# Scores of the first batch from undivided float32 over 64 rows, and one ring of seven staging buffers

## The chip, the cores and the metric

The kernel runs on one core of a Trainium2 chip. The metric is the device time of one execution in microseconds (us). Five engines work side by side, each through its own list of instructions in order: TensorE (PE, with its weight loads shown as PEld), VectorE (DVE), ScalarE (ACT), GpSimd (POOL) and SyncE (SP), which here issues nearly all DMAs.

## The reference, cut to what matters

Three stages follow each other: attention that keeps only the 32 largest scores of a row, a dense feed-forward layer, and a mixture of eight experts with two of them for each token.

```python
def _attn_ref(q, k, v):                        # (4 batches, 8 heads, 576, 64)
    scores = scale * np.matmul(q, k.transpose(0, 1, 3, 2))
    kth = np.partition(scores, -top_k, axis=-1)[..., -top_k:-top_k + 1]   # top_k = 32
    scores = np.where(scores >= kth, scores, -1000000000.0)
    ...
    return np.matmul(attn, v)

def reference(**kwargs):
    attn_out = _attn_ref(**attn_kwargs)
    x = attn_out.transpose(0, 2, 1, 3).reshape(B * S, H * D)    # 2304 x 512
    x = _moe_ref(x=x, **moe_kwargs)      # max(x @ w_in, 0)**2 @ w_out, inner width 2048
    return _moe2_ref(x=x, **moe2_kwargs)  # top 2 of 8 experts, inner width 1024
```

## The kernel before, in words

**Attention.** Work goes by units: one tile of 128 queries and one pair of heads; the 64 queries that are left of each batch's 576 make smaller "left" units. Batch 0 has units 0 to 19 of 80, the last four of them left units. For each head of a unit TensorE makes a score tile of 128 x 576 (line 439, in `scores`), ScalarE copies it out (442), VectorE searches it for its 32 largest values (453 to 494, some 28 instructions a head), ScalarE and GpSimd make the mask and the exponent (506 to 512), TensorE transposes (523) and multiplies by V (564).

**Divided operands.** TensorE's fp32r products take a reduced float32, so q and k are divided in a high part (ScalarE, line 400) and a low rest (line 401, VectorE or GpSimd, in `split`). The 64 rows of a head stand twice over the 128 partitions: `prep_k` puts the high part of k in rows 0 to 63 and its rest in rows 64 to 127, `prep_q` makes one tile of the high part of q and one of its rest, each over all 128 rows. A score tile is the sum of two fp32r products over 128 rows, each in two halves of 288 columns: four matmuls a head. The undivided k arrives in `kn` (two buffers, line 409), the undivided q in `qn` (two buffers, line 424). For batch 0 the first four heads of k and the first and third load of q are divided on VectorE, the rest on GpSimd.

**The feed-forward layer beside it.** Its weights arrive as 64-bit words and are turned to float32 by `convert`, 32 times: a load into `raw` (four buffers, line 147), two passes on ScalarE (153, 157), two on VectorE (155, 156), one on GpSimd (158), and a store to `whole` (159). The layer runs in chunks of token tiles. Chunk 0 (tiles 0 and 1) uses `whole` as plain float32 (loads at 333, products at 351 and 315). Chunk 1 loads `whole` again into `raw` (336), divides it (340, 341) and stores the parts in `wsc` (342), which the later chunks load.

**Order.** The program is written with priorities; a scheduler fixes each engine's list beforehand. Between the pieces of a unit the feed-forward matmuls of the chunk that is due are put in by a pace that counts them. SP issues DMAs in the order of its list, and an issue that has to wait for a buffer holds all behind it. The zero fills of `xs` and `out` (lines 136, 139) and the conversions stand on the same list as the loads of q, k and v. When attention is over, the rest of the feed-forward layer and then the experts run on TensorE.

Of the kernel before, what the change touches and what calls it, by code (L numbers as in the profile page):

```python
# [32 lines left out]
LAST_WAIT = 8  # L33
EXPERT_WAIT = 60
EARLY = 3
SOON = 300
# [18 lines left out]
def attention_ffn_moe(ctx: ExitStack, tc: tile.TileContext, q, k, v, w_ffn, w_route, noise, w_exp, out,  # L55
# [86 lines left out]


    def convert(vpool, f, which):
        n = DM
        raw = vpool.tile([P, 2 * n], U32, name="raw", bufs=4 if keep is not None else 2)
        nc.sync.dma_start(raw, w_ffn[f, which])
# [153 lines left out]
    def ffn(t0, nt, xT):  # L301
# [24 lines left out]
        for f in range(NF):  # L326
# [7 lines left out]
            elif divide:  # L334
                raw = vpools[0].tile([P, 2 * DM], U32, name="raw", bufs=4 if keep is not None else 2).bitcast(F32)
                nc.sync.dma_start(raw, whole[f].rearrange("p a d -> p (a d)"))
                for i, (w, eng) in enumerate(((wi, nc.gpsimd), (wo, nc.vector))):
                    part = raw[:, i * DM:(i + 1) * DM]
                    with prompt():
                        nc.scalar.activation(w[:, 0, :], part, AF.Copy)  # L340
                        eng.tensor_tensor(w[:, 1, :], part, w[:, 0, :].bitcast(F32), op=ALU.subtract)
                    nc.sync.dma_start(wsc[f][:, i], w.bitcast(F32))
            else:
                nc.sync.dma_start(wi.bitcast(F32), wsc[f][:, 0])
                nc.sync.dma_start(wo.bitcast(F32), wsc[f][:, 1])
# [57 lines left out]
    def prep_k(b, g, j):  # L403
# [3 lines left out]
        for h in ([2 * j], [2 * j + 1]) if (b, g) == (0, 0) else ([2 * j, 2 * j + 1],):  # L407
            kn = apool.tile([P, 2, S], F32, name="kn", bufs=2)[:, 0:len(h), :]
            nc.sync.dma_start(kn, k[b, 4 * g + h[0]:4 * g + h[-1] + 1].rearrange("h p s -> p h s"))
            dst = K4[b, g][:, h[0]:h[-1] + 1, :]  # L410
            for i in range(len(h)):
                split(nc.vector if (b, g) == (0, 0) else nc.gpsimd, dst[:, i], dst[:, i], kn[:, i], D)

# [7 lines left out]
    def prep_q(b, g, s0):  # L421

        qn = apool.tile([P, 4, P], F32, name="qn", bufs=2)
        nc.sync.dma_start(qn.rearrange("p h s -> p (h s)"), q[b, s0 // P, g])
        qt = apool.tile([P, 2, 4, P], F32R, name="qt", bufs=3)
        split(nc.vector if b == 0 and s0 == 0 else nc.gpsimd, qt[:, 0], qt[:, 1], qn, 0)
        return qt

    def scores(pairs, sb, whole, then):


        ps = ps_s.tile([P, 2, 512], F32, name="ps")
        for i, (st, kt, par) in enumerate(pairs):
            for n in range(2):
                if whole:
                    at, w = n * HS, HS
                else:
                    at, w = ((LEFT * par, NFULL * P), (0 if par else NFULL * P, LEFT))[n]
                nc.tensor.matmul(ps[:, n, 0:w], st, kt[:, at:at + w], start=(i == 0), stop=(i == len(pairs) - 1))  # L439
        with tc.high_priority(SOON):  # L440
# [127 lines left out]
    def pair_full(b, j, qt):  # L568

        hA = 2 * j  # L570
        q0 = 2 * (j % 2)
        sm = apool.tile([P, 2], F32, name="sm", bufs=6)
        e = apool.tile([P, 2 * S], F32, name="sb", bufs=4)
        for i in range(2):
            kt = K4[b, j // 2][:, (hA + i) % 4]
            sb = e[:, i * S:(i + 1) * S]
            scores([(qt[:, 0, q0 + i, :], kt, i), (qt[:, 1, q0 + i, :], kt, i)], sb, True,
                   lambda w, m, sb=sb, one=sm[:, i:i + 1]: softmax(sb, w, m, one))
            yield
# [9 lines left out]
    def pair_left(b, j, qt):  # L589
        hA = 2 * j  # L590
        q0 = 2 * (j % 2)
        st = []
        for i in range(2):
            kt = K4[b, j // 2][:, (hA + i) % 4]
            st += [(qt[:, 0, q0 + i, :], kt, i), (qt[:, 1, q0 + i, :], kt, i)]
        sm = apool.tile([P, 2], F32, name="sm", bufs=6)
# [7 lines left out]

        scores(st, e, False, then)
        yield
# [521 lines left out]
```

## Time and profile before

| | us |
|---|---|
| median of 3 runs | 1338.55 (1336.74 to 1340.67) |
| the profiled execution | 1336.86 |
| its span in the trace | 1335.1 |
| PE busy, share of the span | 1241.5 (93%) |
| DVE busy | 899.2 (67%) |
| ACT busy | 856.6 (64%) |
| POOL busy | 746.2 (56%) |

The busy time of a whole span says little here, since the stages have different limits: VectorE is the fullest engine in the first 200 us, TensorE from about 400 us on. The rest of the profile is read by stretch: the slices of the page, the busy time of each engine in stretches of 50 us, then the instructions around the places that the change touches, and what they waited for.

### The profile page before, as it was taken

How to read it: one execution, taken by the hardware profiler on the slowest of the kernel's cores; microseconds unless marked ns; L12 is line 12 of the kernel's file. 1: busy time of each engine (PE TensorE's matmuls, PEld its weight loads, DVE VectorE, ACT ScalarE, POOL GpSimd, SP SyncE). 2: the span in 40 equal slices, each digit the busy share in tenths (PEclk: the TensorE clock that was granted, in tenths of full speed). 3: DMA queues.
4: the chain of work that ended last, by engine and by line, in shares of the span. 5: the costliest groups of instructions: out<-in, count | busy, mean ns of one | idle time of the engine just before them, and what ended most of it. 6: DMA issues, size and time to landing. Idle time of an engine off the chain costs nothing.

```text
span 1335.1 us, 26136 instructions
## 1 busy us (share of the span) xinstructions
PE 1241.5 (93%) x8030; PEld 1071.8 (80%) x8030; DVE 899.2 (67%) x4557; ACT 856.6 (64%) x1886; POOL 746.2 (56%) x1243
## 2 busy tenths in 40 slices
PE   3769889989998999999999999999999999999997
PEld 2556667777887888888888888899899999988886
DVE  8999989998986899978677410255534343444554
ACT  6878879989897889987878653543433333332443
POOL 5857798887786676767655635333432241503221
PEclk9889999999999999999999999999999999999999
DMA  9998886875675554366534689366643443534464
GB/s 333 361 368 292 274 273 235 309 260 181 219 231 193 166 174 157 106 211 204 168 115 158 205 297 332 113 198 197 192 151 117 143 136 119 174 103 143 141 202 140
DMA packets 93302, 270.06 MB, mean 202 GB/s; under 512 B 11612, under 2 KB 11740, under 8 KB 93152
## 3 DMA queue, kind: packets, MB, share of 16 engines
q1 hardware_dynamic: 83872, 239.91, 54.3%
q0 software_dynamic: 9280, 28.40, 5.9%
q8 instruction: 65, 1.06, 0.3%
q14 instruction: 85, 0.70, 0.2%
HBM read 209.90 MB, written 60.45 MB: 202 GB/s over the span
## 4 chain that ended last, share of the span: by engine, by line
PE 61%; ACT 13%; DVE 11%; DMA 7%; issue 5%; POOL 3%; SPq 0%; POOLq 0%; DVEq 0%; ACTq 0%
PE pa L564 5%; PE ph L693 5%; PE ph L695 4%; PE ph L694 4%; PE acc L676 4%; PE acc L674 4%; PE acc L675 4%; PE ps L439 4%; PE pa L523 3%; PE acc L322 3%; PE acc L320 3%; PE acc L321 3%; DMA raww<-in_exp 3%; PE pf L357 2%; PE pf L358 2%
## 5 line engine op out<-in xcount | busy, mean ns | idle before, releaser
L511 POOL TENSOR_TENSOR sb<-sb,w 128x576 f32<-128x576 f32 x144 | 205.8, 1430 | 63.3 <-ACT w L510 59.3
L453 DVE MAX8 m<-sb 128x8 f32<-128x115 f32 (+1 forms) x720 | 190.3, 264 | 53.1 <-ACT sb L442 47.6
L457 DVE MATCH_REPLACE8 w<-m,sb 128x115 f32<-128x115 f32 (+1 forms) x720 | 187.1, 263 | 0.0
L699 ACT ACTIVATE ht<-ph 128x384 fp32r<-128x384 f32 (+1 forms) x128 | 55.8, 436 | 195.2 <-PE ph L695 177.0
L715 POOL DMA_INDIRECT out<-y,info x40 | 45.1, 1127 | 242.4 <-DVE y L714 224.7
L439 PE MATMUL ps<-K,qt 128*128 128x288 f32 (+2 forms) x640 | 131.4, 333 | 43.9 <-ACT sb L442 30.0
L700 DVE SCALAR_TENSOR_TENSOR ht<-ph,ht 128x384 fp32r<-128x384 f32 (+1 forms) x128 | 62.7, 490 | 161.7 <-ACT ht L699 148.5
L693 PE MATMUL ph<-xe,wi 128*128 128x256 f32 (+1 forms) x512 | 159.9, 312 | 1.9 <-ACT wi L686 1.0
L695 PE MATMUL ph<-xe,wi 128*128 128x256 f32 (+1 forms) x512 | 159.2, 311 | 0.2 <-DVE wi L687 0.2
L694 PE MATMUL ph<-xe,wi 128*128 128x256 f32 (+1 forms) x512 | 158.9, 310 | 0.0
L439 PEld LDWEIGHTS ps<-K,qt 128*128 128x128 f32 x640 | 103.7, 204 | 64.4 <-ACT sb L442 37.7
L512 ACT ACTIVATE sb<-sb,keep 128x576 f32<-128x576 f32 x144 | 112.5, 781 | 28.1 <-POOL sb L511 27.6
L674 PE MATMUL acc<-wo,ht 128*128 128x512 f32 x320 | 125.8, 397 | 0.4 <-DVE y L714 0.4
L675 PE MATMUL acc<-wo,ht 128*128 128x512 f32 x320 | 125.3, 395 | 0.0
L510 ACT ACTIVATE w<-sb,keep 128x576 f32<-128x576 f32 x144 | 111.3, 775 | 16.4 <-POOL keep L506 16.2
L371 POOL TENSOR_TENSOR gt<-r,gt 128x384 fp32r<-128x384 f32 (+1 forms) x96 | 90.7, 946 | 53.2 <-ACT gt L370 39.9
L481 DVE MAX8 m<-w 128x8 f32<-128x288 f32 x288 | 116.0, 443 | 0.1
L357 PE MATMUL pf<-xT,wi 128*128 128x384 f32 (+1 forms) x320 | 106.0, 331 | 5.4 <-ACT r L364 3.9
L523 PE MATMUL pa<-ident,sb 128*128 128x128 f32 x576 | 94.8, 289 | 16.5 <-ACT sb L512 7.1
L676 PE MATMUL acc<-wo,ht 128*128 128x512 f32 x320 | 108.9, 401 | 0.0
L525 ACT COPY pt<-pa 128x512 f32<-128x512 f32 x144 | 83.2, 578 | 32.1 <-PE pa L523 21.2
L693 PEld LDWEIGHTS ph<-xe,wi 128*128 128x128 f32 x512 | 96.4, 188 | 8.5 <-ACT wi L686 1.4
(211 smaller groups left out, 3511.9 us busy)
## 6 DMA issues: line engine op xcount, KB each, us to landing
raww<-in_exp SPq DMA_DIRECT2D x88, 512.0 KB
wi<-wsc SPq DMA_DIRECT2D x64, 512.0 KB
wo<-wsc SPq DMA_DIRECT2D x64, 512.0 KB
raw<-in_ffn SPq DMA_DIRECT2D x32, 512.0 KB
xs<-xr SPq DMA_DIRECT2D x40, 258.0 KB
mr<-xs SPq DMA_DIRECT2D x40, 258.0 KB
qn<-in_q SPq DMA_DIRECT2D x40, 256.0 KB
whole<-ca SPq DMA_DIRECT2D x32, 256.0 KB
```

What stands on the lines that cost most here:

```text
L357: nc.tensor.matmul(ph[:, 0:n], wi[:, 0, sl], xT[:, 0, c, 0:n], start=(c == 0), stop=False)
L439: nc.tensor.matmul(ps[:, n, 0:w], st, kt[:, at:at + w], start=(i == 0), stop=(i == len(pairs) - 1))
L453: in_turn(nc.vector.max(parts[i][1], sb[:, parts[i][0]]))
L457: in_turn(nc.vector.match_replace(out=w[:, sl], in_to_replace=top, in_values=sb[:, sl], imm_value=NEG))
L511: nc.gpsimd.tensor_tensor(sb, sb, w, op=ALU.subtract)
L523: nc.tensor.transpose(pt[:, c * P:(c + 1) * P], e[:, c * P:(c + 1) * P], ident)
L674: queued(nc.tensor.matmul(acc[t], hs[i][:, 0, sl], wo[:, 0, :], start=(f == 0), stop=False))
L675: queued(nc.tensor.matmul(acc[t], hs[i][:, 0, sl], wo[:, 1, :], start=False, stop=False))
L676: queued(nc.tensor.matmul(acc[t], hs[i][:, 1, sl], wo[:, 0, :], start=False, stop=(f == NFE - 1)))
L693: queued(nc.tensor.matmul(ph[:, 0:n], wi[:, 0, sl], xe[i][:, 0, c, :], start=(c == 0), stop=False))
L694: queued(nc.tensor.matmul(ph[:, 0:n], wi[:, 0, sl], xe[i][:, 1, c, :], start=False, stop=False))
L695: queued(nc.tensor.matmul(ph[:, 0:n], wi[:, 1, sl], xe[i][:, 0, c, :], start=False, stop=(c == NC - 1)))
```

## The change

For batch 0 (`WHOLE_BATCHES = 1`) q and k are loaded undivided straight into the tiles that TensorE reads, `qt` and `K4`, and nothing of them is divided. A head's score tile is one plain float32 product over 64 rows in place of two fp32r products over 128; its two halves of columns are taken from different rows, the first from rows 0 to 63 and the second from rows 64 to 127, where q and k stand twice. The later batches are computed as before. Their q and k, and the `raw` tiles of the conversions and of chunk 1, now take their staging buffers from one ring of seven tiles of 4 KB a partition (`staged`); before, `raw` had four of them, `kn` two of 4.5 KB and `qn` two of 2 KB. k of the later batches is loaded one head at a time instead of two.

```diff
+WHOLE_BATCHES = 1
+    def staged():
+        return vpools[0].tile([P, 2 * DM], U32, name="raw", bufs=7 if keep is not None else 4)
     def convert(vpool, f, which):
-        raw = vpool.tile([P, 2 * n], U32, name="raw", bufs=4 if keep is not None else 2)
+        raw = staged()
             elif divide:
-                raw = vpools[0].tile([P, 2 * DM], U32, name="raw", bufs=4 if keep is not None else 2).bitcast(F32)
+                raw = staged().bitcast(F32)
     def prep_k(b, g, j):
-            kn = apool.tile([P, 2, S], F32, name="kn", bufs=2)[:, 0:len(h), :]
-            nc.sync.dma_start(kn, k[b, 4 * g + h[0]:4 * g + h[-1] + 1].rearrange("h p s -> p h s"))
             dst = K4[b, g][:, h[0]:h[-1] + 1, :]
+            src = k[b, 4 * g + h[0]:4 * g + h[-1] + 1].rearrange("h p s -> p h s")
+            if b < WHOLE_BATCHES:
+                nc.sync.dma_start(dst.bitcast(F32), src)
+                continue
             for i in range(len(h)):
-                split(nc.vector if (b, g) == (0, 0) else nc.gpsimd, dst[:, i], dst[:, i], kn[:, i], D)
+                kn = staged().bitcast(F32)[:, 0:S]
+                nc.sync.dma_start(kn, src[:, i])
+                split(nc.gpsimd, dst[:, i], dst[:, i], kn, D)
     def prep_q(b, g, s0):
-        qn = apool.tile([P, 4, P], F32, name="qn", bufs=2)
+        qt = apool.tile([P, 2, 4, P], F32R, name="qt", bufs=3)
+        if b < WHOLE_BATCHES:
+            nc.sync.dma_start(qt[:, 0].bitcast(F32).rearrange("p h s -> p (h s)"), q[b, s0 // P, g])
+            return qt
+        qn = staged().bitcast(F32)[:, 0:4 * P].rearrange("p (h s) -> p h s", h=4)
         nc.sync.dma_start(qn.rearrange("p h s -> p (h s)"), q[b, s0 // P, g])
-        qt = apool.tile([P, 2, 4, P], F32R, name="qt", bufs=3)
-        split(nc.vector if b == 0 and s0 == 0 else nc.gpsimd, qt[:, 0], qt[:, 1], qn, 0)
+        split(nc.gpsimd, qt[:, 0], qt[:, 1], qn, 0)
+    def products(b, j, qt, i):
+        kt = K4[b, j // 2][:, (2 * j + i) % 4]
+        at = 2 * (j % 2) + i
+        if b < WHOLE_BATCHES:
+            return [(qt[:, 0, at, :].bitcast(F32), kt.bitcast(F32), i)]
+        return [(qt[:, 0, at, :], kt, i), (qt[:, 1, at, :], kt, i)]
     def scores(pairs, sb, whole, then, in_halves):
-                nc.tensor.matmul(ps[:, n, 0:w], st, kt[:, at:at + w], start=(i == 0), stop=(i == len(pairs) - 1))
+                rows = slice(n * D, (n + 1) * D) if in_halves else slice(0, P)
+                nc.tensor.matmul(ps[:, n, 0:w], st[rows], kt[rows, at:at + w], start=(i == 0), stop=(i == len(pairs) - 1))
```

The scheduler moves other work with it. On SP, from the start of its list, before (K is a tile of k, L136 and L137 are zero fills):

```order
L424 DMA qn<-in_q 128x512
L409 DMA kn<-in_k 128x576 x2
L418 DMA vt<-in_v 128x512 x5
L125 DMA wg<-in_route 128x64
L409 DMA kn<-in_k 128x576
L126 DMA nz<-in_noise 128x144
L409 DMA kn<-in_k 128x576
L424 DMA qn<-in_q 128x512 x2
L147 DMA raw<-in_ffn 128x1024 x4
L136 DMA xs<-xr 128x516 x4
L409 DMA kn<-in_k 128x2x576
```

and with the change:

```order
L433 DMA qt<-in_q 128x512
L415 DMA K_117<-in_k 128x576 x4
L415 DMA K_235<-in_k 128x2x576 x2
L426 DMA vt<-in_v 128x512 x5
L126 DMA wg<-in_route 128x64
L127 DMA nz<-in_noise 128x144
L433 DMA qt<-in_q 128x512 x2
L151 DMA raw<-in_ffn 128x1024 x7
L137 DMA xs<-xr 128x516 x5
```

All eight heads of k stand ahead of v, and seven loads of the conversions are issued in a row instead of four.

On PE, the end of chunk 0, from the products with V of unit 14 to those of unit 15, before:

```order
L564 MATMUL pa<-pt,vt 64x128 x8
L523 MATMUL pa<-ident,sb 128x128 x4
L315 MATMUL acc<-wo,gt 128x512 x2
L523 MATMUL pa<-ident,sb 128x128 x4
L351 MATMUL pf<-xT,wi 128x256 x4
L315 MATMUL acc<-wo,gt 128x512 x2
L550 MATMUL pa<-ident,sb 128x128
L351 MATMUL pf<-xT,wi 128x256 x4
L315 MATMUL acc<-wo,gt 128x512 x2
L439 MATMUL ps<-K_1973,qt 128x288 x4
L551 MATMUL pa<-ident,rb 128x128
L315 MATMUL acc<-wo,gt 128x512
```

and with the change (351, 315, 439, 523 and 564 are now 355, 319, 459, 543 and 584):

```order
L584 MATMUL pa<-pt,vt 64x128 x8
L543 MATMUL pa<-ident,sb 128x128 x4
L319 MATMUL acc<-wo,gt 128x512 x2
L355 MATMUL pf<-xT,wi 128x256 x4
L319 MATMUL acc<-wo,gt 128x512 x2
L543 MATMUL pa<-ident,sb 128x128 x4
L570 MATMUL pa<-ident,sb 128x128
L571 MATMUL pa<-ident,rb 128x128
L319 MATMUL acc<-wo,gt 128x512
L459 MATMUL ps<-K_1871,qt 128x288 x4
```

Four matmuls of the first layer and two of the second have gone from this piece to the unit before it.

On DVE, the start of its list, from its first work on q and k, before:

```order
L401 TENSOR_TENSOR qt<-qn,qt 128x512
L401 TENSOR_TENSOR K_120<-kn,K_120 64x576 x2
L453 MAX m<-sb 128x8 x2
...
L401 TENSOR_TENSOR K_120<-kn,K_120 64x576
L484 TENSOR_SCALAR low<-m 128x5x11
...
L401 TENSOR_TENSOR K_120<-kn,K_120 64x576
L489 MAX low_164<-low 128x8
L453 MAX m<-sb 128x8
L401 TENSOR_TENSOR qt<-qn,qt 128x512
```

With the change the six instructions of line 401 are gone and the list begins with the search (L473 MAX is L453 before):

```order
L972 CAST first<-row_i 128x1
L473 MAX m<-sb 128x8 x2
L477 MATCH_REPLACE w<-m,sb 128x116
L473 MAX m<-sb 128x8
L477 MATCH_REPLACE w<-m,sb 128x115
```

## Rows read from the trace of the kernel before

**Rows 1.** The page's slices: busy tenths of 40 equal slices, granted clock, DMA share.

```profile
PE   3769889989998999999999999999999999999997
DVE  8999989998986899978677410255534343444554
PEclk9889999999999999999999999999999999999999
DMA  9998886875675554366534689366643443534464
```

**Rows 2.** Busy us of each engine by stretch, clock, DMA share, GB/s.

```profile
core 0: us, PE busy (x) PEld busy (x) DVE busy (x) ACT busy (x) POOL busy (x), PEclk, DMA share, GB/s
0.00:50.00 50.00, 23.11 (x116) 17.94 (x116) 44.56 (x234) 37.41 (x69) 31.91 (x57) 1.00 1.00 347
50.00:100.00 50.00, 32.09 (x211) 25.65 (x212) 50.00 (x324) 40.17 (x86) 33.78 (x41) 0.76 1.02 362
100.00:150.00 50.00, 45.51 (x265) 32.80 (x262) 50.00 (x239) 43.25 (x97) 36.05 (x38) 0.96 0.86 281
150.00:200.00 50.00, 44.02 (x220) 30.22 (x219) 43.75 (x218) 39.72 (x92) 42.77 (x43) 0.93 0.82 276
200.00:250.00 50.00, 46.86 (x376) 38.77 (x374) 47.55 (x289) 47.12 (x113) 43.55 (x78) 1.00 0.74 264
```

**Rows 3.** What DVE waited for, 8 to 190 us: total, times, longest.

```profile
DVE m L453 <- ACT sb L442: 0.7, 2, 0.4
```

**Rows 4.** DVE's timeline, 0 to 14 us: start, duration, instruction, [idle before, releaser].

```profile
4.97 0.76 DVE L401 TENSOR_TENSOR K<-kn,K 64x576 fp32r<-64x576 f32 x1
7.83 0.46 DVE L453 MAX8 m<-sb 128x8 f32<-128x116 f32 x2 [0.41 <-ACT sb L442]
11.18 0.76 DVE L401 TENSOR_TENSOR K<-kn,K 64x576 fp32r<-64x576 f32 x1
12.46 0.76 DVE L401 TENSOR_TENSOR K<-kn,K 64x576 fp32r<-64x576 f32 x1
13.56 0.68 DVE L401 TENSOR_TENSOR qt<-qn,qt 128x512 fp32r<-128x512 f32 x1
```

**Rows 5.** The chain that ended last, its first links: start, us, what.

```profile
1.24 3.00 DMA kn<-in_k
4.26 0.69 ACT K L400
...
5.78 1.34 PE ps L439 x4
7.15 0.66 ACT sb L442
```

**Rows 6.** Line 401 over the whole run: min/median/max ns of one.

```profile
L401 POOL TENSOR_TENSOR qt<-qn,qt x38: 1262/1292/1801, 13.6 to 691.5; 128x512 fp32r<-128x512 f32 x38
L401 POOL TENSOR_TENSOR K<-kn,K x28: 1402/1416/1595, 25.0 to 534.8; 64x576 fp32r<-64x576 f32 x28
```

**Rows 7.** PE's timeline, 130 to 160 us.

```profile
147.02 0.79 PE L439 MATMUL ps<-K,qt 128*128 128x288 f32 x4 [0.59 <-ACT sb L442]
147.74 0.44 PE L564 MATMUL pa<-t,vt 128*64 128x128 f32 x4
148.01 1.04 PE L564 MATMUL pa<-pt,vt 128*64 128x128 f32 x16
152.69 1.56 PE L439 MATMUL ps<-K,qt 128*128 128x512 f32 x8 [1.31 <-ACT sb L442]
```

**Rows 8.** What DVE waited for, 190 to 206 us.

```profile
DVE sm L518 <- ACT sm L517: 5.3, 3, 2.5
DVE m L453 <- ACT sb L444: 1.7, 1, 1.7
```

**Rows 9.** PE's timeline, 186 to 206 us.

```profile
194.06 1.89 PE L351 MATMUL pf<-xT,wi 128*128 128x256 f32 x8
195.79 1.88 PE L315 MATMUL acc<-wo,gt 128*128 128x512 f32 x4
197.50 0.27 PE L550 MATMUL pa<-ident,sb 128*128 128x128 f32 x1
```

**Rows 10.** What SP's queue waited for, 0 to 300 us.

```profile
SPq L342 <- POOL wi L341: 18.4, 9, 4.3
SPq L342 <- DVE low L492: 14.8, 5, 5.4
SPq L342 <- DVE wo L341: 14.2, 5, 5.3
```

**Rows 11.** The chain that ended last, a load of chunk 1.

```profile
243.72 4.69 DMA raw<-whole
```

More of the change, by code (lines that the diff above doesn't have):

```diff
@@ L421, in prep_q, with scores @@
     def prep_q(b, g, s0):
-        qn = apool.tile([P, 4, P], F32, name="qn", bufs=2)
+        qt = apool.tile([P, 2, 4, P], F32R, name="qt", bufs=3)
[3 more added lines that the diff above has]
+        qn = staged().bitcast(F32)[:, 0:4 * P].rearrange("p (h s) -> p h s", h=4)
         nc.sync.dma_start(qn.rearrange("p h s -> p (h s)"), q[b, s0 // P, g])
-        qt = apool.tile([P, 2, 4, P], F32R, name="qt", bufs=3)
-        split(nc.vector if b == 0 and s0 == 0 else nc.gpsimd, qt[:, 0], qt[:, 1], qn, 0)
-        return qt
-    def scores(pairs, sb, whole, then):
+        split(nc.gpsimd, qt[:, 0], qt[:, 1], qn, 0)
+        return qt
+    def products(b, j, qt, i):
[4 more added lines that the diff above has]
+        return [(qt[:, 0, at, :], kt, i), (qt[:, 1, at, :], kt, i)]
+    def scores(pairs, sb, whole, then, in_halves):
         ps = ps_s.tile([P, 2, 512], F32, name="ps")
@@ L570, in pair_full @@
         hA = 2 * j
-        q0 = 2 * (j % 2)
         sm = apool.tile([P, 2], F32, name="sm", bufs=6)
@@ L574, in pair_full @@
         for i in range(2):
-            kt = K4[b, j // 2][:, (hA + i) % 4]
             sb = e[:, i * S:(i + 1) * S]
-            scores([(qt[:, 0, q0 + i, :], kt, i), (qt[:, 1, q0 + i, :], kt, i)], sb, True,
-                   lambda w, m, sb=sb, one=sm[:, i:i + 1]: softmax(sb, w, m, one))
+            scores(products(b, j, qt, i), sb, True,
+                   lambda w, m, sb=sb, one=sm[:, i:i + 1]: softmax(sb, w, m, one), b < WHOLE_BATCHES)
             yield
@@ L590, in pair_left @@
         hA = 2 * j
[L591 to L595, printed above, removed]
+        st = products(b, j, qt, 0) + products(b, j, qt, 1)
         sm = apool.tile([P, 2], F32, name="sm", bufs=6)
@@ L603, in then @@
                 left_keys(lf, i, e)
-        scores(st, e, False, then)
+        scores(st, e, False, then, b < WHOLE_BATCHES)
         yield
```

## The prediction

> **What bounds the kernel now.** I began with the slices of the page [rows 1]: VectorE is full in the first 200 us, TensorE from the middle on. The change works on the first batch only, so the stretches of the first 250 us come next [rows 2]: from 50 to 150 us VectorE is busy for all of 100.00 us, while TensorE rests for 17.9 and 4.5, and ScalarE and GpSimd for 7 to 16 us in each 50. What VectorE waited for between 8 and 190 us is 0.7 us in all [rows 3]. So up to 190 us the time is VectorE's work and the moment at which it starts; GpSimd, ScalarE and most of TensorE run in its shade. From 190 to 206 us it is otherwise: VectorE waits for 5.3 + 1.7 = 7.0 us on ScalarE [rows 8], and ScalarE on scores and transposes that stand on TensorE between the last products of chunk 0 [rows 9]. In the 50 us after that the four engines are busy for 43 to 48 us each [rows 2], and from the middle on TensorE alone is full [rows 1]. Nothing there belongs to batch 0; I take it that a shift at 200 us is carried to the end.
>
> **The change part by part.**
>
> Start. The first search begins at 7.83 us [rows 4]. Before it: k lands at 4.26, ScalarE copies (0.69), VectorE makes the rest (4.97 to 5.73), TensorE multiplies from 5.78 (1.34) and ScalarE copies out from 7.15 [rows 4, 5]. With the change TensorE can start when k has landed, 4.26 instead of 5.78: 1.5 us earlier, if its four passes take what the four took before. That is the first unknown: no row shows a product over 64 rows. A plain float32 matmul shows as two records; eight of 256 columns take 195.79 - 194.06 = 1.73 us, 0.216 each [rows 9], so 0.243 for 288 columns. A score tile has four. If the two halves, on different rows, run side by side, two in a row count, 0.49 us; if one after the other 0.97. The tail of a group is 1.89 - 1.73 = 0.16 [rows 9], which makes 0.65 or 1.13; the four fp32r products before take 0.79 with theirs [rows 7]. At the start everything on TensorE was slower by 1.34 / 0.79 = 1.7, so 1.1 or 1.9 against 1.34. The gain at the start is thus between 1.5 - 0.6 = 0.9 and 1.5 + 0.2 = 1.7. I take 1.5, near the upper end, since the nearest row is the product with V: its matmuls fill 64 columns of the array in pairs, and 16 records of 128 columns take 1.04 us [rows 7] where 16 times 0.108 in a row would be 1.73; 8 times 0.108 and the tail are 1.02, so they run in pairs.
>
> The Trainium skill says the same of rows (TensorE: Matmul & The Clock Gate, Part 3: matmuls on distinct row groups run concurrently); no row here shows it; by it the sum is the 5.4 below. Against the change speaks another page of the Trainium skill (TensorEngine Tiling (Array Packing), Key Properties): changing the tiling mode drains the array, and each score tile of batch 0 would now enter and leave such a mode. The products with V do so too, and rows 7 leave them 0.02 us for it; by this row the sum stays. By a drain as long as a tail, twice for each of 36 tiles, TensorE would lose 11.5 us, about what the bad case below takes, and the time would be that of the first rival.
>
> VectorE's divisions. Six go; three lie before the first search and are in the 1.5 above. The other three are 0.76 + 0.76 + 0.68 = 2.2 us [rows 4], in a stretch without rest: all behind them moves by 2.2 us. Both bounds are 2.2.
>
> GpSimd's and ScalarE's divisions. GpSimd loses four of k at 1.42 and eight of q at 1.29 = 16.0 us [rows 6], ScalarE eight of 0.69 [rows 5] and ten of q of about as much, some 12 us. The cover is VectorE's full stretch: on the path 0. If it were not full, this would be worth up to GpSimd's share, but rows 3 leave no room.
>
> TensorE's scores. 32 full heads cost 0.65 or 1.13 instead of 0.79 us, -0.14 or +0.34. A left unit takes 1.56 now [rows 7]; then it has two heads with two passes of 512 columns at 0.43, 1.73 and the tail, 1.9, or 2.1 with the passes of 64 columns in a row: +0.3 to +0.55 for each of four. In the worst case 10.9 + 2.2 = 13 us on an engine that rests for 55 us of the first 200 [rows 2]; between 100 and 200 us it is 2.7 (units 12 to 15) + 2.2 = 4.9 against 10.5. Mostly hidden; in the bad case I charge a third, 1.6 us, in the good one nothing.
>
> The end of chunk 0. The order takes a group of four matmuls of the first layer (1.73 us) and two of the second (four records, 197.50 - 195.79 = 1.71 us [rows 9]) out of the stretch in which VectorE waits, and puts them a unit earlier, where TensorE has rest. At best VectorE's 7.0 us of waiting shrinks by 3.4; at worst the next thing is as late (the scores of the next unit, behind the same softmax) and it is 0. Neither end has a nearer row; I take half, 1.7.
>
> The ring. Seven loads of the conversions in flight instead of four; in the first 100 us the DMA engines are at 1.00 to 1.02 of their time [rows 2], so it only reorders what lands. The bytes are the same, twelve more issues on SP's list. q of batch 0 now waits for a qt buffer instead of a qn; VectorE works about two units behind the scores, which hides a late q. I count 0, with bounds below.
>
> Sum: 1.5 + 2.2 + 1.7 = 5.4 us. The profiled execution took 1336.86 us, so 1331.5 for it. It lies 1.7 below the median; on the median the forecast is 1338.55 - 5.4 = **1333.2 us**. Its own bounds: 0.9 + 2.2 = 3.1 (1335.5) to 1.7 + 2.2 + 3.4 = 7.3 (1331.3).
>
> **The rivals.** About 0.3% (4 us) is what a measurement of this kernel can tell from no change: faster is below 1334.5, slower above 1342.6.
>
> No change. The halves do not run side by side, so the change doesn't do what its 64 rows promise: 0.9 + 2.2 + 1.7 - 1.6 = 3.2, that is 1335.4, and what the later stretches don't carry on brings it nearer to 1338.55. For it: 64-row products are in no row, and after 200 us three engines compete, so a shift may get lost. Against: TensorE's rest in rows 2.
>
> Slower, by the ring. SP issues in order, and now loads of k and q of batch 1, `raw` of chunk 1 and the conversions wait for the same seven buffers in turn. Place: 200 to 300 us, where chunk 1 divides its weights. There SP's stores already wait 18.4 + 14.8 + 14.2 us for lines 341 and 492 [rows 10]. If a load of q or k waits for a buffer that an undivided `raw` holds, the loads and stores behind it are late by a landing of 4.69 us [rows 11]. One such wait is lost in the slack; three that reach TensorE's products of chunk 1 cost 14.1: 1338.55 - 5.4 + 14.1 = 1347. Two give 1342.5, the edge; it decides from three on. For it: one queue, one ring. Against: chunk 1's loads have seven places instead of four, and that makes them earlier, not later.
>
> Faster still, by the ring. For the same reason the load of 4.69 us that stands on the chain [rows 11] is issued earlier and leaves it: 1333.2 - 4.7 = 1328.5.
>
> **How the numbers follow.** The forecast 0.46, the deeper ring on top 0.12: faster 0.58. No change 0.27. Slower by the ring 0.15. The predicted time is the likeliest case's, 1333.2. For eight in ten the range leaves out what lies below 1327 (the faster rival with its upper end, half of it) and the worse half of the slower rival: 1327 to 1344.
>
> **What would show it.** Right: the first MAX8 at about 6.3 us (6.9 if the halves run in a row); the four records of a score tile in about 0.65 us with starts in pairs; VectorE without rest up to some 186 us and then with clearly less than 7.0 us of waiting; batch 0 over 4 to 6 us earlier, and the same distance at the start of the experts. GpSimd's busy time falls by 16, ScalarE's by 12, VectorE's by 4.4 us. Wrong: VectorE waits in the first 190 us for scores or for SP's loads of q; issues on SP between 150 and 300 us that stand longer than before and TensorE waiting for weights of chunk 1; or batch 0 that ends earlier while the end of attention does not move.

## The result, and the profile after

The changed kernel takes 1354.62 us in the median (1353.48 to 1357.53), the kernel before 1339.61 beside it: the ratio on record is 1.0121, interval 1.0097 to 1.0144 (the quotient of the two medians, 1.0112, lies inside it; ratios below are those on record too). It is slower by 15 to 16 us where 5.4 us less were forecast. The profiled execution took 1353.48 us, its span is 1351.8.

The page of the changed kernel, busy time of each engine and the slices (as in [rows 1]):

```profile
PE 1253.4 (93%) x8030; PEld 1063.8 (79%) x8030; DVE 894.4 (66%) x4551; ACT 848.3 (63%) x1868; POOL 728.5 (54%) x1231
...
PE   4768999887998999999999999999999999999997
DVE  8999969997796799988767610255544443443554
```

VectorE has 4.8 us less to do, ScalarE 8.3 and GpSimd 17.7: the work that was to go has gone, and the time went up all the same. Busy us by stretch, as in [rows 2], with two stretches more:

```profile
50.00:100.00 50.00, 36.57 (x212) 23.58 (x212) 49.82 (x311) 37.04 (x77) 26.85 (x34) 0.75 1.00 353
100.00:150.00 50.00, 42.86 (x231) 27.36 (x232) 50.00 (x237) 41.87 (x92) 32.53 (x35) 0.90 0.86 289
150.00:200.00 50.00, 45.51 (x214) 28.07 (x211) 39.43 (x207) 36.03 (x85) 42.53 (x48) 0.93 0.77 255
200.00:250.00 50.00, 46.37 (x365) 37.84 (x364) 45.14 (x281) 44.02 (x106) 37.10 (x67) 1.00 0.66 233
...
300.00:350.00 50.00, 40.72 (x311) 34.24 (x310) 31.28 (x200) 39.12 (x97) 37.74 (x67) 0.93 0.60 201
```

Up to 150 us VectorE is as full as before. From 150 to 200 us it has 39.43 where it had 43.75, and from 300 to 350 us only 31.28, where the kernel before has 41.91. Where time is lost shows best in the units. For each kernel I took the start of the first product with V (line 564 before, 584 now) of every unit from the trace, and subtract that of the kernel before. Each column comes from one profiled execution of each kernel: `e6_before_wait` and `e6b_before_full`, which run the same order up to 292 us, differ by 1.4 and 1.6 us at units 7 and 16, so an offset of 2 us or less says nothing by itself. The last columns are the median time and the ratio to runs of the kernel before beside it; the kernels below the first line are those of the experiments.

| kernel | unit 7 | 16 | 26 | 29 | 44 | 79 | us | ratio |
|---|---|---|---|---|---|---|---|---|
| before, at (us) | 99.0 | 209.4 | 300.7 | 323.5 | 451.5 | 772.5 | | |
| the change | -7.2 | +3.5 | +1.5 | +16.5 | +15.9 | +15.6 | 1354.6 | 1.0121 |
| e1_plain_only | -12.1 | +0.2 | -3.7 | +5.8 | +12.1 | +9.8 | 1347.3 | 1.0072 |
| e2_ring_only | +2.8 | +11.1 | +9.8 | +25.3 | +25.7 | +24.5 | 1357.6 | 1.0147 |
| e3_k_apart | -7.6 | -0.9 | -0.6 | 0.0 | +0.4 | -1.2 | 1336.4 | 1.0006 |
| e4_q_apart | -6.4 | +2.5 | +4.5 | +8.1 | +8.0 | +5.5 | 1345.5 | 1.0064 |
| e5_k_early | -6.4 | +7.2 | +11.5 | +12.2 | +19.2 | +19.3 | 1353.4 | 1.0100 |
| e6_before_wait | +1.2 | -0.4 | +3.5 | +3.3 | +2.8 | +2.3 | 1340.8 | 1.0025 |
| e6b_before_full | -0.2 | -2.0 | -1.7 | -1.6 | -2.1 | -2.4 | 1336.2 | 0.9997 |
| e7_before_light | +1.1 | +1.2 | +5.6 | +7.4 | +6.7 | +4.7 | 1347.8 | 1.0070 |
| e8_k_apart_light | -7.1 | -5.4 | -9.9 | -1.1 | -3.6 | -6.9 | 1337.3 | 0.9996 |

The change loses twice. Its units are 6 to 9 us ahead up to unit 7 and 3.5 behind at unit 16 (100 to 210 us); they lose 15 us more between units 26 and 29 (300 to 325 us). In this kernel what stands at unit 44 is carried to unit 79 unchanged. For the first loss, what VectorE waited for between 182 and 207 us (over these 25 us the kernel before shows 8.2 in all, 7.0 of it in [rows 8]):

```profile
DVE m L473 <- ACT sb L464: 4.7, 2, 4.5
DVE wo L345 <- ACT wo L344: 4.7, 1, 4.7
DVE sm L538 <- ACT sm L537: 4.0, 1, 4.0
DVE w L477 <- POOL sb L531: 0.9, 1, 0.9
```

That is 14.3 us. For the second loss, GpSimd's timeline from 295 us and, last, the row of VectorE that ends it:

```profile
295.89 1.22 POOL L276 DMA_INDIRECT xs<-xr,si  x1 [0.92 <-DVE x L556]
297.41 0.97 POOL L276 DMA_INDIRECT xs<-xr,si  x1 [0.31 <-issue]
298.69 0.97 POOL L276 DMA_INDIRECT xs<-xr,si  x1 [0.30 <-issue]
299.97 0.96 POOL L276 DMA_INDIRECT xs<-xr,si  x1 [0.30 <-issue]
305.50 1.39 POOL L405 TENSOR_TENSOR K<-raw,K 64x576 fp32r<-64x576 f32 x1 [4.57 <-DMA xs<-xr,si]
306.97 2.76 POOL L531 TENSOR_TENSOR sb<-sb,w 128x576 f32<-128x576 f32 x2
...
308.40 0.09 DVE L477 MATCH_VALUE_LOAD w<-m,sb 128x8 f32 x1 [6.18 <-POOL sb L531]
```

The four scatters send chunk 0's routed rows to `xs` (lines 272 to 276). The next instruction on GpSimd is the division of a head of k of batch 2, and it stands still for 4.57 us until the scatters have landed; behind it waits the mask of a search, and for that VectorE waits 6.18 us. In the kernel before the four divisions of this half of k ran from 193.9 to 199.4 us, and nothing waits behind the scatters.

The wait goes on to TensorE, and something more stands behind it there. TensorE rests for 4.90 us, and then the granted clock is at its lower level: 0.51 from 310 to 317 us (1.2 GHz nearly throughout), where the kernel before shows 1.00. First that stretch and the one ahead of it in the change, then the same stretch in the kernel before, then three rows of the change: a product of line 325 takes 0.39 us ahead of the rest and 0.63 behind it. The lower clock lasts for 6.8 us; at half the speed that is at most 3.4 us of TensorE's work, an estimate from these rows.

```profile
300.00:310.00 10.00, 5.39 (x50) 1.00 0.56 190
310.00:317.00 7.00, 5.89 (x19) 0.51 0.40 141
```

```profile
310.00:317.00 7.00, 7.00 (x68) 1.00 0.32 113
```

```profile
299.47 0.39 PE L325 MATMUL acc<-wo,gt 128*128 128x512 f32 x1
310.29 1.08 PE L543 MATMUL pa<-ident,sb 128*128 128x128 f32 x4 [4.90 <-DVE x L556]
314.08 0.63 PE L325 MATMUL acc<-wo,gt 128*128 128x512 f32 x1
```

The built program shows why a division of k waits there at all: after scatters, the first GpSimd subtraction over half the rows (64) is made to wait for their landing, while those over 128 rows (q, masks, weights) are not. The two runs with an added instruction below show the same.

### The profile page after: what moved, and what is told of

Read it like the earlier page. It is cut to its first block, busy times and chain, and to the rows that moved or that the text cites. A ratio compares the mean times of both kernels' runs of the same rounds, so it can differ in the third digit from the quotient of the medians.

```text
span 1351.8 us, 26081 instructions
## 1 busy us (share of the span) xinstructions
PE 1253.4 (93%) x8030; PEld 1063.8 (79%) x8030; DVE 894.4 (66%) x4551; ACT 848.3 (63%) x1868; POOL 728.5 (54%) x1231
## 4 chain that ended last, share of the span: by engine, by line
PE 57%; DVE 16%; issue 8%; ACT 7%; DMA 6%; POOL 5%; SPq 0%; POOLq 0%; DVEq 0%; ACTq 0%
PE pa L584 5%; DVE w L477 4%; PE ps L459 4%; PE ph L707 4%; PE ph L709 4%; PE ph L708 4%; PE acc L688 4%; PE acc L689 4%; PE acc L690 3%; PE acc L326 3%; PE acc L324 3%; PE acc L325 3%; PE pa L543 3%; DVE m L473 3%; PE pf L361 3%
## 5 line engine op out<-in xcount | busy, mean ns | idle before, releaser
L473 DVE MAX8 m<-sb 128x8 f32<-128x115 f32 (+1 forms) x720 | 190.2, 264 | 55.1 <-ACT sb L462 41.8
L459 PE MATMUL ps<-K,qt 128*128 128x288 f32 (+5 forms) x640 | 132.3, 377 | 37.9 <-ACT sb L462 26.8
L459 PEld LDWEIGHTS ps<-K,qt 128*128 128x128 f32 (+1 forms) x640 | 89.8, 200 | 63.9 <-ACT sb L462 37.4
L361 PE MATMUL pf<-xT,wi 128*128 128x384 f32 (+1 forms) x320 | 104.9, 328 | 0.7 <-ACT r L368 0.7
L362 PE MATMUL pf<-xT,wi 128*128 128x384 f32 (+1 forms) x320 | 101.8, 318 | 0.0
```

The source lines that it names most:

```text
L361: nc.tensor.matmul(ph[:, 0:n], wi[:, 0, sl], xT[:, 0, c, 0:n], start=(c == 0), stop=False)
L459: nc.tensor.matmul(ps[:, n, 0:w], st[rows], kt[rows, at:at + w], start=(i == 0), stop=(i == len(pairs) - 1))
L473: in_turn(nc.vector.max(parts[i][1], sb[:, parts[i][0]]))
```

## The experiments

### The two parts apart

The scores part with the buffers of before (`kn` 2, `qn` 2, `raw` 4):

```diff
-                kn = staged().bitcast(F32)[:, 0:S]
+            kn = apool.tile([P, 2, S], F32, name="kn", bufs=2)[:, 0:len(h), :]
...
-        qn = staged()...
+        qn = apool.tile([P, 4, P], F32, name="qn", bufs=2)
-        ... name="raw", bufs=7
+        ... name="raw", bufs=4
```

> The scores part of the change alone: batch 0's scores are plain and undivided, but k, q and the conversions are staged in the buffers of the kernel before (kn 2, qn 2, raw 4). Theory (the loss comes from staging k in the shared ring: the division of k of batch 2 stands behind the four scatters on GpSimd and waits for their landing, +11 us at 297 to 320 us, and the shift of k of batch 1 costs a further few us before 200 us): without the ring nothing of this is left, k of batch 2 is divided near 194 us as before, and the 7 to 9 us won by unit 7 are largely carried to the end, 1330 to 1335 us (ratio 0.993 to 0.997). Rival A (the plain, undivided scores themselves make the loss, because VectorE and the conversions get out of step): 1348 to 1356 us, as the whole change.

And the ring alone (`WHOLE_BATCHES = 0`, divisions on the engines of before):

> The ring part of the change alone: batch 0 is divided as in the kernel before (WHOLE_BATCHES 0, on the same engines), but k (one head at a time), q and the conversions share the ring of seven. Theory (k in the ring): three of four divisions of k of batch 2 stand behind the scatters and wait for their landing; the loss of 11 us at about 300 us appears again, and nothing is won at the start: 1348 to 1356 us (ratio 1.008 to 1.013). Rival A (the scores part makes the loss): 1336 to 1341 us, no change.

Measured: 1.0072 (1.0045 to 1.0099) for the scores, 1.0147 (1.0120 to 1.0173) for the ring. The ring alone costs what the theory said and a little more (1357.6 us), with both losses in the table. But the scores alone did not win 5 us, they lost 10 to 11, against the theory and just short of rival A's range, and without any ring. Their loss between units 26 and 29 looks different. VectorE's timeline of this kernel, two rows, and then GpSimd's over the same time:

```profile
303.47 6.02 DVE L345 TENSOR_TENSOR wo<-raw,wo 128x512 fp32r<-128x512 f32 x1 [1.60 <-ACT wo L344]
309.41 0.20 DVE L504 TENSOR_SCALAR low<-m 128x55 f32<-128x55 f32 x1
```

```profile
302.85 0.72 POOL L375 TENSOR_TENSOR gt<-r,gt 128x256 fp32r<-128x256 f32 x1
303.55 0.29 POOL L568 TENSOR_SCALAR rb<-sm 128x128 f32<-128x128 f32 x1
303.82 1.29 POOL L405 TENSOR_TENSOR qt<-qn,qt 128x512 fp32r<-128x512 f32 x1
305.07 0.45 POOL L562 TENSOR_TENSOR xT<-x,xT 128x128 fp32r<-128x128 f32 x1
305.49 0.19 POOL L526 TENSOR_TENSOR keep<-m,cb 128x4 f32<-128x4 f32 x1
305.64 0.72 POOL L375 TENSOR_TENSOR gt<-r,gt 128x256 fp32r<-128x256 f32 x1
306.32 1.39 POOL L531 TENSOR_TENSOR sb<-sb,w 128x576 f32<-128x576 f32 x1
307.68 1.26 POOL L405 TENSOR_TENSOR qt<-qn,qt 128x512 fp32r<-128x512 f32 x1
311.76 0.20 POOL L526 TENSOR_TENSOR keep<-m,cb 128x4 f32<-128x4 f32 x1 [2.82 <-DVE m L514]
```

A weight division on VectorE that takes 0.67 us at its quickest (0.81 in the middle of this kernel's sixteen) takes 6.02. It begins while GpSimd works off what had gathered behind its scatters, and it ends 0.5 us after GpSimd has come to rest at 308.94. Every search behind it on VectorE is late by 5.4 us. Here too the granted clock is at its lower level behind it, from 308.6 to 315.4 us.

### Who in the ring

k in its two own buffers, ring of five for the rest; and q in its own, ring of six for the rest:

```diff
-    ... name="raw", bufs=7
+    ... name="raw", bufs=5
-                kn = staged().bitcast(F32)[:, 0:S]
+            kn = apool.tile([P, 2, S], F32, name="kn", bufs=2)[:, 0:len(h), :]
...
```

> The whole change, but k has the two kn buffers of the kernel before, of two heads each; q and the conversions share a ring of five. Theory (k in the ring is the cause): no division of k of batch 2 waits for a scatter, time as that of the scores part alone, 1330 to 1336 us. Rival B (any sharing of the ring with the conversions' and chunk 1's weight loads costs, whoever shares): 1343 us or more. Rival A: 1348 to 1356 us.

> The whole change, but q has the two qn buffers of the kernel before; k and the conversions share a ring of six. Theory (k in the ring): one division of k of batch 2 still stands a few instructions behind the scatters and waits for their landing, so most of the loss stays: 1345 to 1356 us. Rival B' (q in the ring is the cause, since the loads of q come most often): 1330 to 1336 us.

Measured: 1.0006 (0.9988 to 1.0023) with k apart and 1.0064 (1.0039 to 1.0089) with q apart. With k taken out of the ring the whole loss is gone; with q taken out about half of it. So k costs more than q in these builds; but k apart is no gain either, though its units are 7.6 us ahead at unit 7. What k's place in the ring does is seen in when GpSimd divides it. Line 405 over the whole run, the change and then k apart:

```profile
L405 POOL TENSOR_TENSOR K<-raw,K x24: 1389/1422/1967, 163.4 to 550.8; 64x576 fp32r<-64x576 f32 x24
```

```profile
L405 POOL TENSOR_TENSOR K<-kn,K x24: 1393/1417/1863, 36.3 to 535.1; 64x576 fp32r<-64x576 f32 x24
```

With its own buffers the first half of batch 1's k is divided from 36.3 us on; in the ring it stands behind all loads of the conversions and comes at 163.4, and batch 2's comes at 287 to 317 instead of 189 to 195.

How many of the four divisions of this half of batch 2's k stand behind the scatters goes with the second loss. With three of them there, units 26 to 29 lose 15.0 us in the change, 15.5 with the ring alone, and 13.2 in the other order of the change further below. With q apart one is left there, and they lose 3.6; with k apart none is, and they lose 0.6. (The scores alone lose 9.5 there, with the hold shown above, and a kernel further below 8.8 with another.) In the three with the large loss TensorE rests for 4.90, 4.85 and 4.71 us and then stands at the lower clock, for 6.8, 10.2 and 10.2 us in all between 290 and 330 us; with q apart and k apart the granted clock is 1.00 all through these 40 us.

### The place behind the scatters

The change, with batch 2's first half of k asked for twelve units earlier:

```diff
-            todo.setdefault(last - AHEAD - at + 2, []).append((prep_k, ...
+            todo.setdefault(last - AHEAD - at + 2 - (12 if b == 2 and n < 2 else 0), []).append((prep_k, ...
```

> The whole change, ring of seven and all, but the loads of the first half of batch 2's keys are asked for twelve units earlier, so that their four divisions stand on GpSimd well before chunk 0's scatters (none of them waits for a scatter any more). Theory (the division behind the scatters costs the 10 us at 297 to 320 us): that step is gone from the unit times, 1341 to 1347 us. Rival B (the shared ring itself costs, wherever the division stands): 1350 to 1357 us.

Measured: 1.0100 (1.0071 to 1.0130). The step at units 26 to 29 is gone (+11.5 to +12.2, where the change goes from +1.5 to +16.5): the place was right. But the time did not come back, it is in the range of rival B. The four divisions now run at 197 to 209 us, at the end of chunk 0, and at unit 23 this kernel is already 9 us further behind than the change (+12.9 against +4.1). At unit 29 it is 4.3 us better than the change, and from there to unit 44 it loses 7.0 us more. Its VectorE between 182 and 212 us:

```profile
DVE wo L345 <- ACT wo L344: 7.8, 1, 7.8
DVE m L473 <- ACT sb L464: 4.5, 1, 4.5
```

What the wait by itself costs, in the kernel before, with one addition of one column behind chunk 0's scatters, over 64 rows and over 128. The orders of the two are the same on all engines; against the kernel before a few instructions change places on VectorE and ScalarE, so not quite nothing else moves:

```diff
+        if t0 == 0:
+            half = fpool.tile([P, 1], F32, name="pad", bufs=1)
+            with tc.issue_after(slot_writes[-1].ins), tc.high_priority(PROMPT):
+                nc.gpsimd.tensor_tensor(half[64:P], sf[64:P, 1, 0:1], sf[64:P, 1, 1:2], op=ALU.add)
```

> The kernel before with one instruction more: a GpSimd addition of one column on 64 rows, put directly behind the four scatters of chunk 0, where the program makes it wait for their landing as it does with the key division of the changed kernel. Nothing else moves. Theory (the wait for the landing is what costs): GpSimd rests about 4.5 us there and its train of work behind it is late by that, VectorE and TensorE wait in turn, 1340 to 1346 us, 4 to 10 us more than before. Rival (such a wait is absorbed, the loss needs the divisions themselves, 1.4 us each, among the chunk's own GpSimd work): 1334 to 1339 us.

> The same one-column GpSimd addition behind chunk 0's scatters, at the same place of the same order, but on 128 rows, where the program does not make it wait for the scatters' landing. If the wait of the half-height form is what cost 3.5 us: 1336 to 1339 us, as the kernel before, and 2 to 5 us below the half-height one. If the instruction or the order that came with it cost them: 1340 to 1342 us again.

Measured: 1.0025 (1.0008 to 1.0043) over 64 rows and 0.9997 (0.9985 to 1.0010) over 128. GpSimd's last scatter and the addition, first over 64 rows, then over 128:

```profile
292.34 0.97 POOL L272 DMA_INDIRECT xs<-xr,si  x1 [0.30 <-issue]
296.82 0.19 POOL L278 TENSOR_TENSOR pad<-rs 64x1 f32<-64x1 f32 x1 [3.50 <-DMA xs<-xr,si]
```

```profile
290.96 0.97 POOL L272 DMA_INDIRECT xs<-xr,si  x1 [0.30 <-issue]
291.96 0.20 POOL L278 TENSOR_TENSOR pad<-rs 128x1 f32<-128x1 f32 x1
```

A wait of 3.50 us on GpSimd makes the units late by 3.9 (from -0.4 at unit 25 to +3.5 at unit 26), and most of it arrives at the end. Nothing there took up this delay of GpSimd. TensorE is in it as above: it rests for 4.09 us until 298.13 us, and from 297.8 to 301.1 us the granted clock is 0.50, where the run over 128 rows has 1.00 from 290 to 325 us. But this is a quarter of the 15 us. In the change three divisions and their loads stand in the same 30 us, and the clock is low for twice as long; how the 15 us divide between these was not tried.

### Less work for TensorE

```diff
+                if plain and f % 2 and f < NF - 1:
+                    continue
                 if plain:
                     with behind():
                         nc.tensor.matmul(acc[tt], gt[:, 0, sl].bitcast(F32), wo[:, 0, :].bitcast(F32),
```

> The kernel before without 14 of the 64 second-layer products of chunk 0 (odd blocks of hidden columns but the last are left out, so the output of these rows is not the reference's); that is 14 x 0.6 us = 8.4 us less for TensorE between 110 and 205 us and nothing less for VectorE. Theory P (TensorE bounds the stretch from 100 to 205 us, so what VectorE wins before it is spent in waiting there): 6 to 9 us less than before, 1327 to 1331 us. Rival V (VectorE bounds that stretch until the conversions end): 1333 to 1337 us, no change.

> The kernel with k's own buffers (the whole change but k not in the ring) without the same 14 of 64 second-layer products of chunk 0. Theory P: TensorE bounded it too, and the relief lets the 4 to 5 us won by VectorE come through besides: 1324 to 1330 us. Rival V: it stays at 1333 to 1338 us, as with all products.

Measured: 1.0070 (1.0047 to 1.0094) and 0.9996 (0.9983 to 1.0010). The edit takes out more than was worked out beforehand: 14 of the 32 products, which is 28 of the 64 records, and the busy time of this line falls from 31.9 to 17.3 us, by 14.6 and not by 8.4. It also changes the pace that counts these products, and so the built order. Neither theory gave the first result, a slower kernel; the second lies in the range of rival V. So the two runs don't tell what bounds the stretch. In the second the relief does come through for a while, the units are 9.9 us ahead at unit 26, and at unit 29 they are 1.1 ahead. There the row of the scores part is back, VectorE and then the end of GpSimd's train:

```profile
295.06 5.69 DVE L347 TENSOR_TENSOR wo<-raw,wo 128x512 fp32r<-128x512 f32 x1
```

```profile
298.81 1.39 POOL L533 TENSOR_TENSOR sb<-sb,w 128x576 f32<-128x576 f32 x1
303.62 0.20 POOL L528 TENSOR_TENSOR keep<-m,cb 128x4 f32<-128x4 f32 x1 [3.42 <-DVE m L516]
```

Again the division ends (300.75) some 0.5 us after GpSimd's last instruction (300.20). In the lighter kernel before, such a division takes 4.04 us at 291.86, where its units go from +1.2 to +5.2 (24 to 25). These are the only three of the twenty kernels with such a division over 2.6 us.

### The same work in another order

The losses so far lay in what happened to stand where. So I changed constants that change no work: `ROUTE_WAIT` (30: after how many feed-forward pieces a chunk's routing goes on) and `LEFT_WEIGHT` (0.6: how many pieces a left unit is given). The scheduler then builds another order.

> A control: the kernel before with ROUTE_WAIT 31 instead of 30, which changes no work at all, only where in the program chunk 0's and later chunks' routing is dealt out; the order on every engine shifts from there on. Theory O (the times of all these kernels are set by how well the built order happens to fit, and the constants of the kernel before were chosen for its own order): 2 to 15 us slower, 1339 to 1352 us. Rival W (the order is not so touchy, the losses seen have each a cause in the change): 1334 to 1339 us.

> A second control: the kernel before with LEFT_WEIGHT 0.62 instead of 0.6 (how many feed-forward pieces are dealt out per left-over unit); no work is changed. Theory O: 2 to 15 us slower, 1339 to 1352 us. Rival W: 1334 to 1339 us.

> The kernel with k's own buffers (the whole change but k not in the ring) with ROUTE_WAIT 24 instead of 30: chunk 0's routing and its scatters come earlier among the feed-forward work. Theory O: the time moves by several us either way, between 1328 and 1350 us; if the 4 to 5 us by which its units are ahead until 290 us get past the scatters, 1330 to 1333 us. Rival W: 1335 to 1338 us as without it.

> The same kernel with ROUTE_WAIT 33, the routing later. Theory O: between 1328 and 1350 us and another time than with 24 or 30. Rival W: 1335 to 1338 us.

> The whole change with LEFT_WEIGHT 0.62 instead of 0.6; no work is changed, and a key division still stands behind chunk 0's scatters (one instruction or so later). Theory O (order sets the time): another time than 1354.6 us by more than 4 us, anywhere from 1338 to 1360 us. Theory K (the shared ring costs its own amount, whatever the order): 1351 to 1357 us.

> The kernel with k's own buffers with LEFT_WEIGHT 0.62: Theory O: anywhere from 1328 to 1352 us, with a fair chance of a time below the kernel before, since its units start out 5 to 9 us ahead. Rival W: 1335 to 1338 us as with 0.6.

> The kernel with k's own buffers with ROUTE_WAIT 31: Theory O: anywhere from 1328 to 1352 us, not tied to the 15 us that the same number cost the kernel before. Rival: if ROUTE_WAIT 31 in itself is a bad value (routing later by one piece), 1348 to 1354 us here too.

> The scores part of the change alone (buffers of the kernel before, 1347.3 us as built) with LEFT_WEIGHT 0.62, which changes no work. Theory O (its 11 us are the order's: one division on VectorE held 6 us by a train of eight GpSimd instructions at 303 us, and a step at 410 to 445 us): the 6 us hold is not there in a new order, its units stand 0 to 7 us behind the kernel before at 450 us instead of 12, 1332 to 1345 us. Rival (plain scores cost 11 us by themselves where the ring is not there): 1345 to 1352 us.

> The kernel with k's own buffers with ROUTE_WAIT 31 for chunk 0 alone and 30 for the others: with 31 for all, its units were 2.3 us ahead of the kernel before at 450 us and lost it after 500 us, where the later chunks' routing had moved. If the later order is as in the kernel with 30, the lead stays: 1332 to 1335 us, 2 to 4 us below the kernel before. If a new order in the first 450 us also deals the later one anew: anywhere from 1333 to 1348 us.

| kernel | constant | unit 16 | 29 | 44 | 79 | us | ratio, interval |
|---|---|---|---|---|---|---|---|
| before | ROUTE_WAIT 31 | -0.8 | +1.6 | +7.5 | +11.8 | 1353.2 | 1.0121 (1.0104 to 1.0138) |
| before | LEFT_WEIGHT 0.62 | -1.5 | +0.1 | -0.6 | +0.3 | 1337.8 | 0.9993 (0.9982 to 1.0004) |
| the change | LEFT_WEIGHT 0.62 | +4.4 | +15.7 | +16.0 | +17.0 | 1355.9 | 1.0143 (1.0122 to 1.0165) |
| scores alone | LEFT_WEIGHT 0.62 | +1.1 | +2.1 | -0.4 | +0.7 | 1339.5 | 1.0021 (1.0006 to 1.0036) |
| k apart | LEFT_WEIGHT 0.62 | -0.4 | +2.9 | +0.2 | +6.3 | 1344.1 | 1.0056 (1.0034 to 1.0078) |
| k apart | ROUTE_WAIT 24 | -0.9 | -0.4 | +11.9 | +17.0 | 1357.1 | 1.0140 (1.0118 to 1.0162) |
| k apart | ROUTE_WAIT 31 | -0.3 | -1.5 | -2.3 | +3.7 | 1343.1 | 1.0033 (1.0016 to 1.0050) |
| k apart | ROUTE_WAIT 33 | -1.0 | -4.0 | -2.4 | +4.9 | 1345.6 | 1.0069 (1.0048 to 1.0090) |
| k apart | ROUTE_WAIT 31, chunk 0 only | +0.6 | -0.9 | -1.7 | -2.3 | 1335.4 | 0.9983 (0.9972 to 0.9995) |

One constant, one step, no work changed: with `ROUTE_WAIT` 31 the kernel before loses 15 us, as much as by the whole change, and just more than theory O allowed; with `LEFT_WEIGHT` 0.62 it loses nothing, as rival W said. k apart spreads over 22 us, with one time (1357.1) above theory O's range. The change itself stayed where theory K had it.

Many of these shifts stand beside a lower granted clock. Between units 44 and 79 the kernel before has no time at the lower clock. The five orders above that lose 4.3 to 7.3 us there (`ROUTE_WAIT` 31 in the kernel before, `LEFT_WEIGHT` 0.62 and `ROUTE_WAIT` 24, 31 and 33 with k apart) have 3.4 to 6.8 us of it; of the other kernels, which move by -3.3 to +1.1, only the lighter kernel before has any (3.4). Between units 29 and 44 the largest losses, 12.3 (`ROUTE_WAIT` 24), 6.9 (k asked for early), 6.3 (scores alone) and 5.9 (`ROUTE_WAIT` 31 in the kernel before), stand beside 17.1, 13.7, 10.2 and 10.2 us at the lower clock, against 3.4 in the kernel before; the others have 0 to 6.8 us of it and lose at most 1.6. The clock follows a rest of TensorE in the rows shown for the change, so it can be a part of the loss or only go with it; no run separates the two.

So a single build tells little about a part of this size, and the parts have to be judged over several orders:

- Scores alone: 1.0072 became 1.0021 as soon as the order was another and the 6 us hold was not in it (its longest such division is then 1.71 us). So most of those 11 us went with the order; 2.5 us are left, and two orders do not tell whether the scores cost anything of their own.
- The change kept its loss: +16.0 at unit 44 again, here with the steps at the same units, and +19.2 in the order with k asked for early. Three orders with k in the ring of seven give 1.0100 to 1.0143, mean 1.0121. Six orders with k apart give 0.9983 to 1.0140, mean 1.0048; with q apart, k in a ring of six, the one order gives 1.0064, inside that spread. At unit 44 five of the six with k apart lie between -2.4 and +0.4.
- So k in the shared ring costs on the mean 0.7%, some 10 us, on top of what another order costs; with so few orders and this spread that is a rough figure. That k apart also has a ring of five instead of seven was not separated from it.

The last line is the only kernel whose interval lies below 1: faster than the kernel before by 0.17%, where 2 to 4 us were hoped for. One such interval among nineteen kernels can be luck.

## Why the prediction was wrong, step by step

**The start: right.** First the groups of scores on TensorE, then the first search on VectorE:

```profile
4.48 1.33 PE L459 MATMUL ps<-K,qt 64*128 64x288 f32 x4 [4.48 <-DMA K<-in_k]
108.73 0.76 PE L459 MATMUL ps<-K,qt 64*128 64x288 f32 x4
175.78 1.98 PE L459 MATMUL ps<-K,qt 64*128 64x512 f32 x8
```

```profile
6.53 0.46 DVE L473 MAX8 m<-sb 128x8 f32<-128x116 f32 x2 [3.15 <-ACT sb L462]
```

The first search begins 1.3 us earlier than in [rows 4], forecast 1.5 (0.9 to 1.7). The halves run side by side: four records take 0.76 us, where 0.65 was worked out for pairs and 1.13 for a row, against 0.79 in [rows 7]; at the start a tile took 1.33 us, as before, where 1.1 was worked out. A left unit takes 1.98 (1.9 to 2.1 forecast). Of the drain that the Trainium skill states for a change of the tiling mode (TensorEngine Tiling (Array Packing), Key Properties) the rows show at most the 0.11 us by which a group is longer than was worked out for pairs; the two tails of 0.16 us each that the prediction supposed for the bad case are not there.

**VectorE's divisions, 2.2 us: right where the ring allows it.** With k apart search 20 (counted from 0, at 99.4 us before) begins 3.9 us earlier, with the scores alone 4.4, near the 1.5 + 2.2 of the sum. In the change the lead at search 20 is 0.1 us. VectorE seems to have spent it on the conversions: by 125 us SP has issued 19 stores of converted weights against 17 before, and the last load of a conversion goes out at 148.5 us instead of 168.4. Seven buffers let the conversions run ahead of the searches; that this took the lead was not tried by itself.

**GpSimd and ScalarE at 0: not contradicted.** Their busy time fell by 17.7 and 8.3 us (16 and 12 forecast, so ScalarE's share was too large). The searches gained about the sum of the start and VectorE's divisions; no run took this work away alone.

**The end of chunk 0, 1.7 us: wrong.** VectorE's waiting grew from 8.2 to 14.3 us instead of shrinking. With the scores alone it is 9.8 and with k apart 11.3: where VectorE comes early it waits the longer there, and the matmuls that were moved a unit earlier did not give that back.

**The ring at 0: the step that failed.** The reason given was that seven buffers only reorder what lands. The ring alone, in its one build, costs a ratio of 1.0147, some 20 us; k in it costs some 10 us on the mean of the orders tried. The seven buffers also set which of three users gets one, in the order in which the program asks, and k asks late: batch 1's first half of k moved from 53.6 to 163.4 us, batch 2's from 193.9 to 287 us and later. There it met GpSimd's scatters. The forecast looked at GpSimd's busy time and at SP's list, and never at GpSimd's list as one in which a division can hold up a mask, nor at what TensorE's rest behind it does to the clock (0.51 after 4.90 us).

**The slower rival: near in place and price by luck, wrong in the mechanism.** It said 200 to 300 us, 14.1 us, and SP's queue behind a landing; the larger loss was at 300 to 325 us, 15 us, and GpSimd's queue behind a landing. SP's stores of chunk 1's weights (line 342, now 346) did not wait longer: 60.6 us in all between 150 and 300 us, 62.8 before. And TensorE waits for no load between 200 and 330 us. The rival had 0.15.

**"A shift at 200 us is carried to the end": the second step that failed.** From unit 44 on it holds for the change (+15.9 to +15.6) and for the single wait (+2.8 to +2.3), but five of the other orders lose 4.3 to 7.3 us there. Between units 16 and 44 it does not hold: k apart is 5.2 us ahead at unit 24 and level at unit 29, the lighter k apart drops from 9.9 to 1.1. Leads mostly don't survive there, and so the 5.4 us did not come through without the ring either (k apart 1.0048 on the mean). A hold of VectorE goes with the second drop, 5.0 of its 8.8 us; what takes the lead of k apart was not found, though 3.4 us at the lower clock (281.5 to 284.9 us) fall into it.

**The chances.** 0.58 for faster rested on 5.4 us of work in a kernel whose order alone moves it by 15. The sum was right about VectorE's work; it left out that the order would be built anew.

What stays open: where the 15 us of `ROUTE_WAIT` 31 come from. Some 6 of them arise between units 29 and 44 and some 4 from there to unit 79, both beside a lower clock; the rest comes after attention. Which rests of TensorE come first there was not followed. And how the first loss of the change, 10.7 us between units 7 and 16, divides between conversions that run ahead and eight divisions of k at 163 to 184 us was argued from times only, and not tried.

## What to carry to other kernels

When buffers of several users go into one ring, write down for each user when its tile is asked for and what stands in front of it; a user that asks late can be delayed by the whole ring, and its work lands in another stretch, on an engine whose list may have no room there. Before believing a few microseconds, change a constant that changes no work and see how far the time moves; a part is judged over several orders. And an engine's busy time says nothing about its list: look for what stands right behind an instruction that waits for a landing. Read the granted clock by stretch in every trace: a new rest of TensorE can come with a slower stretch behind it.

## What the runs showed of the hardware

A two-input subtraction on VectorE took 4.04, 5.69 and 6.02 us (0.67 at its quickest) while GpSimd ran instructions without a rest, in two of the three cases until 0.5 us after the last of them. Of the 320 such divisions of the twenty kernels before 340 us, 158 took 0.75 us or more, and all but one of these (the one of 5.69 us) began while a GpSimd instruction ran; of the 162 shorter ones 94 did. The Trainium skill has the kind of it (SBUF — State Buffer, Who interferes with whom: an instruction of VectorE with two inputs in SBUF and one of GpSimd that reads SBUF exclude each other, and the one that comes second is blocked for the whole of the first). The traces agree on the kind, and go further: the longest hold lasted through eight instructions of GpSimd in a row, not one. No run took GpSimd's work away from such a place to see the hold go.

GpSimd's scatters take 0.96 to 1.22 us each to issue in the change, and an instruction that waits for their landing stood for 4.57 us (the change) and 3.50 us (the added wait) after the last was issued.

Behind rests of TensorE of 4.90, 4.85 and 4.71 us the granted clock stood at its lower level, 1.2 GHz, and in the change a product of 128 x 512 then took 0.63 us instead of 0.39.
